# Routing attention chunks in groups of up to four, with row factors made on chip and another order of the last ranks

## The chip, the cores and the metric

One core of a Trainium2 chip. The metric is the device time of one execution in microseconds (us). A core has five engines that each work through their own queue in order: PE (matmuls), DVE (vector operations), ACT (activations and copies), POOL (general vector work and indirect DMA) and SP (which here only issues DMA). An engine that reaches an instruction whose input isn't ready waits, and everything behind it in its queue waits too.

## The reference, cut to what matters

```python
# 1. linear attention with decay: 4 batches, 8 heads, 768 tokens, 64 dims
state = gamma * state + k_t v_t^T;  y_t = scale * q_t state      # per batch and head
x = y.transpose(0, 2, 1, 3).reshape(3072, 512)
# 2. mixture of experts, one expert of 8 for each token
logits = x @ w_gate;  e_idx = argmax(logits)
gate_w = softmax(logits)[e_idx];  eom = sigmoid(x @ w_output_gate)[e_idx]
out[token] = gate_w * eom * (relu(x[token] @ w1[e_idx]) @ w2[e_idx])
# 3. a gated MLP (512 -> 1536 -> 512) on rms-normalised rows
```

## The kernel before, in words

The kernel has three stages: attention with routing (0 to 173 us of the trace), the experts, and the second MLP. The change is in the first stage alone.

**Attention** runs over 24 chunks of 128 tokens, `CPB` = 6 to a batch. The loop over `n` does, in this order: `load(n + 3)` (SP loads 1 MB of q, k and v into one of four `qkv` buffers), `vscale(n + 1)` (POOL makes `vt`, L451), `qk(n + 1)` (PE L467, then two masked copies `am` on DVE, L474), `rows(n - 1)`, `qs_pv(n)` (PE L490, which reads the state `st`, and L495; DVE multiplies by the row factors `rs` into `xt`, L500), `st_up(n)` (PE L513; half of the state is copied out by ACT, L517, and after it the other half by DVE, L518), and `place(n - 1)`. The first chunk of a batch has no L490, the last no L513.

**Rows and routing.** `rows(n)` multiplies `xt` by weights and gate columns (PE L524); DVE adds up the 16 logits `lg` (L529) and ACT copies the 512-wide `row` out of PSUM (L532). Then the chunk is routed, one chunk at a time: a maximum, a comparison, a second maximum, a one-hot `ohb` and the running counts (DVE, L539 to L544), the exponentials (ACT L545, L549), and in `place` the rank in the expert (PE L555 to L557, three small matmuls), the gate and the slot number (DVE L558 to L565). `place` ends with a multiply of the row by its gate (ACT L588), its store to DRAM (DMA issued by ACT, L589) and a scatter of token numbers into the list `lst` (POOL L579).

**Weights beside it.** After every second chunk an expert's weight tile is split in two parts: ACT copies the high part (L179) and POOL subtracts it (L180, 128x1024).

**The last chunks.** Tokens of the first expert tile are gathered from DRAM by four indirect DMAs (L255). Those of the last three chunks are not stored and gathered but multiplied in by a one-hot matrix (`direct_in`, PE L595, which needs `pt`, `rh` and `rl` of `place`); the gathered ones are transposed (`settle_in`, PE L604). Then come the splits (ACT L263, DVE L264) and the first expert matmul, L285.

The order within each engine is the order of the code; there is no scheduler. Tiles are guarded by semaphores.

Of the kernel before, what the change touches and what calls it, by code (L numbers as in the profile page):

```python
# [9 lines left out]
F32 = mybir.dt.float32  # L10
# [34 lines left out]
EARLY = 4  # L45
SETTLED = 4
# [12 lines left out]
A_END = A_IDS + NCH  # L59
# [12 lines left out]
def shape_constants():  # L72
    g = 1.0 - 2.0 ** (-5.0 - np.arange(H, dtype=np.float64))
    p = np.arange(128)
    c = np.zeros((128, C_END))
    c[:, C_ID:C_ID + 128] = np.eye(128)
    c[:, C_EPS] = 1e-6
    c[:, C_MID] = -1024.0
    a = np.zeros((128, A_END))
    a[:, A_MASK:A_MASK + 128] = p[:, None] <= p[None, :]  # L80
    a[:, A_U:A_U + 128] = p[:, None] < p[None, :]
    t = np.arange(CPB)[None, :, None] * CH + p[:, None, None] + 1.0
    a[:, A_VS:A_VS + CPB * H] = (g[None, None, :] ** (-t)).reshape(128, -1)
# [5 lines left out]
    rs = g[hd] ** ti / np.sqrt(D)  # L89
# [14 lines left out]
def fused_kernel(  # L104
# [311 lines left out]
    with ExitStack() as es:  # L416
# [3 lines left out]
        rp = pool(es, "rowp", 4)  # L420
# [7 lines left out]
        e3 = ap.tile([128, 8], BF16, name="e3")  # L428
# [5 lines left out]
        junk = ap.tile([128, 4, NE], F32, name="junk")  # L434
        prio = ca[:, A_PRIO:A_PRIO + 8]

        a_t, vt_t, am_t, xt_t, row_t, rt, direct = {}, {}, {}, {}, {}, {}, {}
# [82 lines left out]
        def rows(n):  # L520
            xt = xt_t.pop(n)
            for k in range(KB):
# [3 lines left out]
            t = rp.tile([128, DM], F32, name="row", tag="row")  # L526
            row_t[n] = t
            lg = tp.tile([128, 16], F32, name="lg", tag="lg")
            DVE.tensor_reduce(  # L529
                out=lg, in_=v[:, :, :, 128:144].rearrange("p a b j -> p j a b"), axis=AX.XY, op=ALU.add  # L530
# [4 lines left out]
            sc = tp.tile([128, 12], F32, name="sc", tag="sc")  # L535
            col = [sc[:, i:i + 1] for i in range(12)]
            mx, pm, nmx, sm, nz, ez, s1, t1, gw, pos = col[:10]
            ohb = tp.tile([128, NE], BF16, name="ohb", tag="ohb")
            DVE.tensor_reduce(out=mx, in_=lg[:, 0:8], axis=AX.X, op=ALU.max)  # L539
            DVE.scalar_tensor_tensor(out=junk[:, 0], in0=lg[:, 0:8], scalar=mx, in1=prio, op0=ALU.is_ge, op1=ALU.mult)  # L540
            DVE.tensor_scalar(out=nmx, in0=mx, scalar1=-1.0, scalar2=None, op0=ALU.mult)
            DVE.tensor_reduce(out=pm, in_=junk[:, 0], axis=AX.X, op=ALU.max)
            DVE.tensor_scalar(out=ohb, in0=prio, scalar1=pm, scalar2=None, op0=ALU.is_equal)
            DVE.tensor_tensor(out=run_cnt[:, n + 1], in0=run_cnt[:, n], in1=ohb, op=ALU.add)  # L544
            ACT.activation(out=junk[:, 1], in_=lg[:, 0:8], func=AF.Exp, bias=nmx, accum_out=sm)  # L545
            DVE.scalar_tensor_tensor(
                out=junk[:, 2], in0=lg[:, 8:16], scalar=-1.0, in1=ohb, op0=ALU.mult, op1=ALU.mult, accum_out=nz
            )
            ACT.activation(out=ez, in_=nz, func=AF.Exp)  # L549
            rt[n] = (ohb, ez, sm, s1, t1, gw, pos)  # L550

        def place(n):
            ohb, ez, sm, s1, t1, gw, pos = rt.pop(n)
            rk = ps[:, 7, (n % 2) * 8:(n % 2) * 8 + 8]
            PE.matmul(rk, lhsT=oh[0:1], rhs=e3[0:1], start=True, stop=False)  # L555
            PE.matmul(rk, lhsT=oh, rhs=run_cnt[:, n], start=False, stop=False)
            PE.matmul(rk, lhsT=uh, rhs=ohb, start=False, stop=True)  # L557
            DVE.tensor_scalar(out=s1, in0=sm, scalar1=1e-9, scalar2=None, op0=ALU.add)  # L558
            DVE.tensor_scalar(out=t1, in0=ez, scalar1=1.0, scalar2=s1, op0=ALU.add, op1=ALU.mult)
            DVE.scalar_tensor_tensor(  # L560
                out=junk[:, 3], in0=rk, scalar=1.0, in1=ohb, op0=ALU.mult, op1=ALU.mult, accum_out=pos
            )
            DVE.reciprocal(out=gw, in_=t1)
            ii = tp.tile([128, 1], I32, name="ii", tag="ii", bufs=3)
            DVE.tensor_copy(out=ii, in_=pos)  # L565
            t = row_t.pop(n)
            if n >= NCH - NDIRECT:
                pt = dp.tile([128, CAPS[0]], F32R, name="pt", tag="pt")
                DVE.tensor_scalar(out=pt, in0=slots, scalar1=pos, scalar2=None, op0=ALU.is_equal)
                rh = dp.tile([128, DM], F32R, name="rh", tag="rh")  # L570
                rl = dp.tile([128, DM], F32R, name="rl", tag="rl")
                ACT.activation(out=rh, in_=t, func=AF.Copy, scale=gw)
                DVE.scalar_tensor_tensor(out=rl, in0=t, scalar=gw, in1=f32(rh), op0=ALU.mult, op1=ALU.subtract)
                direct[n] = (pt, rh, rl)
            if n < NCH - 1:
                store_row(n, t, gw)
            else:
                row_t[n] = (t, gw)
            ins = POOL.indirect_dma_start(  # L579
                out=lst[:, :], out_offset=bass.IndirectOffsetOnAxis(ap=ii, axis=0), in_=ids[:, n:n + 1], in_offset=None  # L580
# [19 lines left out]
        def settle_in(ks):  # L600
            for k in ks:
                for t0 in range(0, CAPS[0], 128):
                    r = min(128, CAPS[0] - t0)
                    PE.matmul(  # L604
                        ps[:, k, t0:t0 + r], lhsT=xw[0:r, t0 // 128, k * 128:(k + 1) * 128], rhs=ident[0:r, 0:r],
                        start=False, stop=True, skip_group_check=True,
                    )
# [44 lines left out]
        SP.dma_start(out=rs[:, 0], in_=rsc[:, 0])  # L652
# [5 lines left out]
        SP.dma_start(out=rs[:, 1], in_=rsc[:, 1])  # L658
# [3 lines left out]
        DVE.tensor_copy(out=e3, in_=ca[:, A_E3:A_E3 + 8])  # L662
# [8 lines left out]
        ex = Experts(None, None, None, None, None)  # L671
        for n in range(NCH):
# [394 lines left out]
```

## Time and profile before

| what | value |
|---|---|
| median of 3 runs | 1124.92 us (1124.22 to 1126.25) |
| the profiled execution | 1119.29 us, of which its span is 1117.2 us |
| mean granted TensorE clock | 0.986 of full speed |
| busy, share of the span | PE 94%, DVE 49%, ACT 34%, POOL 30% |
| first expert matmul (L285) | at 173.34 us of the span |

Times in the trace are counted from the span's start. The profiled execution is 5.63 us faster than the median of the runs; 2.1 us of its time lie outside the span. A row of a timeline gives start, duration, engine, line and operation, and in brackets how long its engine had been idle and what ended that. The view by windows gives the busy time of each engine in a stretch, then the granted clock, the DMA share and GB/s.

### The profile page before, as it was taken

Reading aid. Unit: us, or ns where it says so; the run is one execution under the profiler, and the core shown is the slowest. Engines: PE = TensorE matmul, PEld = TensorE weight load, DVE = VectorE, ACT = ScalarE, POOL = GpSimd, SP = SyncE. Lnnn points to the kernel's source line nnn. Section 1 sums busy time; section 2 is a strip of 40 time slices with the busy share of each in tenths; the row PEclk is TensorE's granted clock in tenths of the full one; section 3 lists DMA queues with packets and bytes.
Section 4 is the critical chain, followed back from the end, with each engine's and each line's share of the span. In section 5 each row is a group of like instructions: output and inputs, shape, how many; then the busy total and the mean of one; then the engine's idle time right before and its main releaser. Section 6 shows DMA issues by size and latency. Waiting matters only on the chain.

```text
span 1117.2 us, 16379 instructions
## 1 busy us (share of the span) xinstructions
PE 1055.5 (94%) x6393; PEld 982.8 (88%) x6394; DVE 550.9 (49%) x1045; ACT 381.4 (34%) x721; POOL 337.2 (30%) x271
## 2 busy tenths in 40 slices
PE   7788889999999999989899899999999999999995
PEld 6687779989999999978788799999999999999995
DVE  4699963256666676888888831111311112211111
ACT  1344333444444544555555531111311112211111
POOL 3355544556466656332433310000110000200002
PEclk9899989999999999999999999999999999999998
DMA  8999724445446555543343220000210000100001
GB/s 301 229 307 284 204 63 135 123 135 197 155 142 205 182 156 155 171 104 94 114 141 114 85 85 29 1 1 1 64 50 1 1 1 30 57 1 1 1 1 60
DMA packets 47864, 116.74 MB, mean 104 GB/s; under 512 B 12966, under 2 KB 24486, under 8 KB 44962
## 3 DMA queue, kind: packets, MB, share of 16 engines
q1 hardware_dynamic: 39602, 97.05, 28.8%
q0 software_dynamic: 4864, 12.53, 3.2%
q10 hardware_dynamic: 3312, 6.03, 1.6%
q8 instruction: 52, 0.85, 0.3%
q14 instruction: 34, 0.28, 0.1%
HBM read 93.06 MB, written 23.11 MB: 104 GB/s over the span
## 4 chain that ended last, share of the span: by engine, by line
issue 43%; PE 25%; DVE 11%; POOL 3%; DMA 2%; ACT 2%; POOLq 0%; DVEq 0%; SPq 0%; ACTq 0%
PE ps L285 12%; PE ps L298 11%; DVE fb L226 2%; DVE fb L229 2%; POOL out_dram L780 2%; DVE fu L232 1%; DVE fb L223 1%; PE ps L271 1%; DMA out_dram<-ob,perm 1%; DVE a L755 1%; DVE al L757 1%; ACT ah L756 1%; DVE ys L347 1%; PE ps L604 1%; DMA raw<-wm 1%
## 5 line engine op out<-in xcount | busy, mean ns | idle before, releaser
L747 PE MATMUL ps<-zh,w 128*128 128x384 f32 x960 | 255.2, 336 | 2.6 <-DVE hl L292 1.3
L755 DVE TENSOR_TENSOR a<-a,ps 128x384 f32<-128x384 f32 x96 | 52.8, 550 | 320.2 <-PE ps L747 317.7
L180 POOL TENSOR_TENSOR w<-raw,w 128x1024 fp32r<-128x1024 f32 x64 | 154.7, 2426 | 103.0 <-ACT w L179 102.2
L747 PEld LDWEIGHTS ps<-zh,w 128*128 128x128 f32 x960 | 174.6, 188 | 5.7 <-ACT a L754 1.7
L747 PE MATMUL ps<-xh,w 128*128 128x384 f32 x576 | 156.5, 341 | 9.8 <-ACT a L754 7.2
L747 PE MATMUL ps<-zl,w 128*128 128x384 f32 x480 | 161.2, 336 | 0.0
L285 PE MATMUL ps<-xh,w 128*128 128x448 f32 (+7 forms) x512 | 149.6, 353 | 0.1
L765 PE MATMUL ps<-w,ah 128*128 128x512 f32 x564 | 145.5, 393 | 0.2 <-ACT ys L320 0.2
L780 POOL DMA_INDIRECT out_dram<-xw,perm x10 | 9.9, 992 | 423.3 <-ACT xw L778 420.1
L756 ACT ACTIVATE ah<-a 128x384 fp32r<-128x384 f32 x94 | 49.3, 525 | 209.6 <-DVE a L755 209.6
L747 PEld LDWEIGHTS ps<-xh,w 128*128 128x128 f32 x576 | 104.9, 188 | 17.3 <-ACT a L754 11.3
L765 PEld LDWEIGHTS ps<-w,ah 128*128 128x128 f32 x564 | 104.7, 188 | 16.6 <-ACT ys L320 0.6
L754 ACT ACTIVATE a<-ps 128x384 f32<-128x384 f32 x96 | 46.7, 487 | 202.6 <-PE ps L747 202.5
L298 PE MATMUL ps<-hh,w 128*128 128x448 f32 (+7 forms) x512 | 106.6, 350 | 0.0
L285 PEld LDWEIGHTS ps<-xh,w 128*128 128x128 f32 x512 | 95.2, 188 | 3.4
L747 PE MATMUL ps<-xl,w 128*128 128x384 f32 x288 | 96.9, 336 | 0.0
L298 PEld LDWEIGHTS ps<-hh,w 128*128 128x128 f32 x512 | 93.8, 188 | 2.9
L747 PEld LDWEIGHTS ps<-zl,w 128*128 128x128 f32 x480 | 90.1, 188 | 2.3
L285 PE MATMUL ps<-xl,w 128*128 128x448 f32 (+7 forms) x256 | 89.8, 351 | 0.0
L180 POOL TENSOR_TENSOR w<-fu,w 128x512 fp32r<-128x512 f32 x36 | 55.7, 1546 | 111.7 <-ACT w L179 108.2
L765 PE MATMUL ps<-w,al 128*128 128x512 f32 x282 | 80.1, 392 | 0.0
L757 DVE TENSOR_TENSOR al<-a,ah 128x384 fp32r<-128x384 f32 x94 | 52.5, 558 | 55.5 <-ACT ah L756 55.5
(154 smaller groups left out, 1497.9 us busy)
## 6 DMA issues: line engine op xcount, KB each, us to landing
raw<-wmoe SPq DMA_DIRECT2D x64, 512.0 KB, 3.9
qkv<-att SPq DMA_DIRECT2D x22, 1024.0 KB, 8.0
raw<-wm SPq DMA_DIRECT2D x36, 512.0 KB, 3.7
xw<-z SPq DMA_DIRECT2D x8, 768.0 KB, 6.4
xr<-row ACTq DMA_DIRECT2D x23, 256.0 KB, 7.8
z<-ys SPq DMA_DIRECT2D x2, 912.0 KB, 7.6
z<-ys SPq DMA_DIRECT2D x2, 896.0 KB, 4.3
z<-ys SPq DMA_DIRECT2D x2, 864.0 KB
```

Source lines behind the costliest of these rows:

```text
L180: POOL.tensor_tensor(out=dst[:, 1, c], in0=src, in1=f32(dst[:, 0, c]), op=ALU.subtract)
L226: DVE.scalar_tensor_tensor(out=b, in0=lo, scalar=29, in1=b, op0=ALU.logical_shift_right, op1=ALU.bitwise_or)
L229: DVE.scalar_tensor_tensor(out=b, in0=hi, scalar=-(1 << 30), in1=b, op0=ALU.bitwise_and, op1=ALU.bitwise_or)
L285: PE.matmul(p, lhsT=wtile[:, s, k * 128:(k + 1) * 128], rhs=x[w % len(xh)][:, k, 0:n], start=(i == 0), stop=(i == 3 * KB - 1),)
L298: PE.matmul(ps[:, 4 + k, 0:n], lhsT=wtile[:, s, 512 + k * 128:512 + (k + 1) * 128], rhs=h, start=(f == 0 and j == 0), stop=(f == NF - 1 an ...
L747: PE.matmul(ps[:, part, 0:BT], lhsT=w2(f, part, s, k * 128, (k + 1) * 128), rhs=zz[:, k], start=(i == 0), stop=(i == 3 * KB - 1),)
L754: ACT.activation(out=a, in_=ps[:, 0, 0:BT], func=AF.Silu)
L755: DVE.tensor_tensor(out=a, in0=a, in1=ps[:, 1, 0:BT], op=ALU.mult)
L756: ACT.activation(out=ah, in_=a, func=AF.Copy)
L757: DVE.tensor_tensor(out=al, in0=a, in1=f32(ah), op=ALU.subtract)
L765: PE.matmul(ps[:, o_bank[b % 2][t]], lhsT=x[:, t * 128:(t + 1) * 128], rhs=w2(f, 2, s, 0, 512), start=(f == 0 and j == 0), stop=(f == NF2 ...
L780: ins = POOL.indirect_dma_start(out=out[:, :], out_offset=bass.IndirectOffsetOnAxis(ap=pm[:, t0 + t], axis=0), in_=o, in_offset=None, boun ...
```

## The change

1. **Groups.** `rows` no longer routes. When the last chunk of a group has its logits, `route` makes a list of steps for the whole group, each step one instruction over up to four chunks (128x32 in place of 128x8), only the running counts one by one. Groups are 4, 4, 4, 4, 3, 2, 2 and 1 chunks. A group of four has 14 steps in a first part and eight in a second, then one `place` per chunk.
2. **Pumps.** The steps wait in a list `todo`. Each iteration takes five of them after `qk(n + 1)` and six after `qs_pv(n)`, 40 from iteration 20 on. For a group of four that ends at chunk e, iteration e+1 has the first six steps, e+2 eleven, e+3 the last of the steps and then all four `place`, ahead of `st_up(e + 3)`.
3. **Formulas.** The accumulated sums of two instructions become reductions of their own, and the exponentials get their maximum subtracted by DVE. A group of four has 19 DVE instructions of routing, a chunk before had 14.
4. **Buffers.** Seven row buffers in place of four; three are tiles that the later stages use.
5. **Row factors.** Five of the six 256 KB loads of `rs` fall away; `rs` of chunk c is the first one times a factor per partition and head pair, four ACT instructions of 128x128 for each c, in iterations 0 to 4.
6. **The last ranks.** `rows` and the first part of the route of chunk 23 stand ahead of all `direct_in`; `settle_in` goes by gathered tiles of 128 tokens (before by blocks of 128 columns); `direct_in` of chunk 22 stands ahead of it.

ACT from the row copy of one iteration (`L532` before, `L542` after) over the stores to the next row copies. Before, over one iteration:

```order
L532 ACTIVATE row<-ps 128x512
L545 ACTIVATE junk,sc<-lg,sc 128x8
L549 ACTIVATE sc<-sc 128x1
L517 ACTIVATE st_134<-ps 64x4x64
L588 ACTIVATE row<-row,sc 128x512
L589 DMA xr<-row 128x512
L532 ACTIVATE row<-ps 128x512
```

After, iteration 6, in which the group of chunks 0 to 3 is placed:

```order
L542 ACTIVATE fu_72<-ps 128x512
L618 ACTIVATE row_136<-row_136,gw_all 128x512
L619 DMA xr<-row_136 128x512
L618 ACTIVATE row_137<-row_137,gw_all 128x512
L619 DMA xr<-row_137 128x512
L618 ACTIVATE row_138<-row_138,gw_all 128x512
L619 DMA xr<-row_138 128x512
L618 ACTIVATE row_139<-row_139,gw_all 128x512
L619 DMA xr<-row_139 128x512
L528 ACTIVATE st_134<-ps 64x4x64
```

Before, the copy of the state stands ahead of one store in each iteration; now it stands behind four in every fourth.

DVE over one iteration. Before, every iteration reads like this (`sc` holds the small values of one chunk):

```order
L474 TENSOR_TENSOR am_661<-ps,ca 128x512
L529 TENSOR_REDUCE lg<-ps 128x16
L539 TENSOR_REDUCE sc<-lg 128x1
L540 SCALAR_TENSOR_TENSOR junk<-lg,sc,ca 128x8
L541 TENSOR_SCALAR sc<-sc 128x1
L542 TENSOR_REDUCE sc<-junk 128x1
L543 TENSOR_SCALAR ohb<-ca,sc 128x8
L544 TENSOR_TENSOR run_cnt<-run_cnt,ohb 128x8
L546 SCALAR_TENSOR_TENSOR junk,sc<-lg,ohb 128x8
L500 TENSOR_TENSOR xt<-ps,rs 128x512
L518 COPY st_133<-ps 64x4x64
L558 TENSOR_SCALAR sc<-sc 128x1
```

After, iteration 6 from its masked copies on (`s_all` is the product under the gate, `gw_all` the gate, `ii_all` the slot number):

```order
L485 TENSOR_TENSOR am_516<-ps,ca 128x512
L583 SCALAR_TENSOR_TENSOR s_all<-sm_all,t_all 128x4
L586 RECIPROCAL gw_all<-s_all 128x4
L556 TENSOR_TENSOR junk_143<-ps,ohb 128x32
L559 TENSOR_REDUCE pos_all<-junk_143 128x4
L589 CAST ii_all<-pos_all 128x4
L539 TENSOR_REDUCE lg<-ps 128x16
L511 TENSOR_TENSOR xt<-ps,rs 128x512
L529 COPY st_134<-ps 64x4x64
```

The gates of four rows are now made ahead of the logits `lg` and of `xt` of that iteration; the iteration behind it has no routing steps.

PE at the end of the attention. Before, between the first `settle_in` and the first expert matmul:

```order
L604 MATMUL ps<-cs,xw 128x128 x3
L604 MATMUL ps<-cs,xw 128x64
L555 LDWEIGHTS oh
L555 MATMUL ps<-e_129,oh 128x8
L556 LDWEIGHTS oh
L556 MATMUL ps<-run_cnt,oh 128x8
L557 LDWEIGHTS uh
L557 MATMUL ps<-ohb,uh 128x8
L604 MATMUL ps<-cs,xw 128x128 x3
L604 MATMUL ps<-cs,xw 128x64
```

After, from the last matmul of chunk 22's `direct_in` on:

```order
L625 MATMUL ps<-pt,rl 128x448
L635 MATMUL ps<-cs,xw 128x128 x8
L562 LDWEIGHTS oh
L562 MATMUL ps<-e_129,oh 128x8
L563 LDWEIGHTS oh
L563 MATMUL ps<-run_cnt,oh 128x8
L564 LDWEIGHTS uh
L564 MATMUL ps<-ohb,uh 128x8
L635 MATMUL ps<-cs,xw 128x128 x4
L635 MATMUL ps<-cs,xw 128x64 x4
L625 MATMUL ps<-pt,rh 128x448
```

The eight matmuls of `direct_in(22)` moved from behind the gathered transposes to ahead of them; the last rank stays between the halves, which are now halves of the tokens.

The core of the diff:

```diff
+GMAX = 4
+GROUPS = [4, 4, 4, 4, 3, 2, 2, 1]
...
+        row_bufs = [rp.tile([128, DM], F32, name=f"row{i}") for i in range(4)] + fl_u + [f32(fl_b[0])]
...
+            first = [
+                red(mx[:, r], lg[:, r, 0:8], ALU.max),
+                tt(j0, lg[:, r, 0:8], mx[:, r].to_broadcast(shape), ALU.is_ge),
+                tt(j0, j0, pr, ALU.mult),
+                red(pm[:, r], j0, ALU.max),
+                tt(ohb[:, r], pr, pm[:, r].to_broadcast(shape), ALU.is_equal),
+                *[tt(run_cnt[:, n + 1], run_cnt[:, n], ohb[:, n], ALU.add) for n in range(n0, n0 + g)],
+                tt(j1, lg[:, r, 0:8], mx[:, r].to_broadcast(shape), ALU.subtract),
+                lambda: ACT.activation(out=j1, in_=j1, func=AF.Exp),
+                tt(j2, lg[:, r, 8:16], ohb[:, r], ALU.mult),
+                red(nz[:, r], j2, ALU.add),
+                lambda: ACT.activation(out=ez[:, r], in_=nz[:, r], func=AF.Exp, scale=-1.0),
+            ]
+            second = [
+                rank,
+                red(sm[:, r], j1, ALU.add),
+                lambda: DVE.tensor_scalar(out=t1[:, r], in0=ez[:, r], scalar1=1.0, scalar2=None, op0=ALU.add),
+                lambda: DVE.scalar_tensor_tensor(
+                    out=s1[:, r], in0=sm[:, r], scalar=1e-9, in1=t1[:, r], op0=ALU.add, op1=ALU.mult
+                ),
+                lambda: DVE.reciprocal(out=gw[:, r], in_=s1[:, r]),
+                tt(j3, rk.rearrange("p (g e) -> p g e", g=g), ohb[:, r], ALU.mult),
+                red(pos[:, r], j3, ALU.add),
+                lambda: DVE.tensor_copy(out=ii[:, r], in_=pos[:, r]),
+                *[lambda n=n: place(n) for n in range(n0, n0 + g)],
+            ]
+            return first, second
...
+                ACT.activation(out=rs[:, c, a], in_=rs[:, 0, a], func=AF.Copy, scale=ca[:, k:k + 1])
...
         for n in range(NCH):
             load(n + 3)
-            if 2 <= n + 2 < CPB:
-                SP.dma_start(out=rs[:, n + 2], in_=rsc[:, n + 2])
...
             qk(n + 1)
+            if n + 1 < CPB:
+                row_scales(n + 1)
+            pump(5)
             if n >= 1:
-                rows(n - 1)
+                routed_rows(n - 1)
             qs_pv(n)
+            pump(6 if n < NCH - 4 else 40)
             st_up(n)
-            if 1 <= n < NCH - 1:
-                place(n - 1)
...
+        routed_rows(NCH - 1)
+        pump(11)
         direct_in(NCH - 3, True)
-        place(NCH - 2)
-        rows(NCH - 1)
+        direct_in(NCH - 2, False)
         settle_in((0, 1))
-        place(NCH - 1)
+        pump(40)
         settle_in((2, 3))
-        direct_in(NCH - 2, False)
         direct_in(NCH - 1, False)
```

`place` loses its rank and gate steps and keeps the scaled row, the store and the scatter.

## Rows read from the trace of the kernel before

**Rows 1.** Windows: busy us of each engine (instructions), granted clock, DMA share, GB/s.

```profile
56.00:84.00 28.00, 24.71 (x327) 22.35 (x322) 26.16 (x90) 12.38 (x30) 15.21 (x17) 1.00 0.98 309
...
196.00:224.00 28.00, 28.00 (x146) 25.69 (x146) 8.13 (x12) 13.24 (x21) 15.08 (x8) 1.00 0.42 127
```

**Rows 2.** Timeline of PE: one iteration without a wait, chunk 21 to 22.

```profile
131.51 1.16 PE L467 MATMUL ps<-qkv 64*128 64x128 f32 x16
...
133.68 1.05 PE L490 MATMUL ps<-qkv,st 128*128 128x128 f32 x8
134.67 1.09 PE L495 MATMUL ps<-am,vt 128*64 128x128 f32 x16
135.59 0.63 PE L513 MATMUL ps<-vt,qkv 128*64 128x64 f32 x16
136.16 0.17 PE L555 MATMUL ps<-e,oh 1*128 1x8 bf16 x1
...
136.40 1.16 PE L467 MATMUL ps<-qkv 64*128 64x128 f32 x16
```

**Rows 3.** DVE in the stretch 0 to 175 us, by line and shape: busy us, mean ns.

```profile
L474 DVE TENSOR_TENSOR am<-ps,ca 128x512 f32<-128x512 f32 x48 | 30.7, 682 | 17.9 <-PE ps L467 17.8
...
L518 DVE COPY st<-ps 64x256 f32<-64x256 f32 x20 | 8.6, 428 | 2.8 <-ACT st L517 2.3
...
L539 DVE TENSOR_REDUCE sc<-lg 128x1 f32<-128x8 f32 x24 | 3.9, 161 | 0.8
```

**Rows 4.** Timelines of POOL and DVE: a split, and two routing steps.

```profile
135.78 2.34 POOL L180 TENSOR_TENSOR w<-raw,w 128x1024 fp32r<-128x1024 f32 x1 [0.87 <-ACT w L179]
138.08 1.04 POOL L451 TENSOR_TENSOR vt<-qkv,ca 128x512 f32<-128x512 f32 x1
...
135.81 2.32 DVE L544 TENSOR_TENSOR run_cnt<-run_cnt,ohb 128x8 bf16<-128x8 bf16 x1
...
156.55 0.23 DVE L540 SCALAR_TENSOR_TENSOR junk<-lg,sc,ca 128x8 f32<-128x8 f32 x1
```

**Rows 5.** Timeline of PE: three starts of L467 (chunks 5, 7, 9).

```profile
32.29 1.16 PE L467 MATMUL ps<-qkv 64*128 64x128 f32 x16
...
50.20 2.08 PE L467 MATMUL ps<-qkv 64*128 64x128 f32 x16 [6.88 <-DMA qkv<-att]
...
61.78 1.16 PE L467 MATMUL ps<-qkv 64*128 64x128 f32 x16
```

**Rows 6.** Waits of SP's queue, 0 to 180 us: us in total, times, longest.

```profile
SPq L445 <- DMA xr<-row: 11.0, 2, 6.5
```

**Rows 7.** DMA issues of the page: times issued, KB, median us to landing.

```profile
qkv<-att SPq DMA_DIRECT2D x22, 1024.0 KB, 8.0
```

**Rows 8.** Timeline of ACT: one row's multiply, and what follows its store's issue.

```profile
86.01 0.72 ACT L588 ACTIVATE row<-row,sc 128x512 f32<-128x512 f32 x1 [1.04 <-DVE ii L565]
...
87.13 1.06 ACT L179 ACTIVATE w<-raw 128x1024 fp32r<-128x1024 f32 x1 [0.40 <-ACT row L588]
```

**Rows 9.** ACT in the stretch 0 to 175 us, by line and shape.

```profile
L532 ACT ACTIVATE row<-ps 128x512 f32<-128x512 f32 x24 | 14.2, 591 | 23.5 <-DVE lg L529 22.6 <-DVE ohb L543 0.5 <-DVE sc L542 0.5
...
L517 ACT ACTIVATE st<-ps 64x256 f32<-64x256 f32 x20 | 7.3, 364 | 1.9 <-PE ps L513 1.9
```

**Rows 10.** A wait of PE in its timeline, and the window of 4 us behind it.

```profile
113.94 0.17 PE L557 MATMUL ps<-ohb,uh 128*128 128x8 bf16 x1 [1.75 <-DVE ohb L543]
...
117.28 1.92 PE L490 MATMUL ps<-qkv,st 128*128 128x128 f32 x8
...
116.00:120.00 4.00, 4.00 (x28) 3.78 (x28) 3.76 (x18) 1.71 (x4) 2.11 (x3) 0.57 0.81 234
```

**Rows 11.** The end of the attention: timelines of DVE and PE.

```profile
152.97 0.69 DVE L500 TENSOR_TENSOR xt<-ps,rs 128x512 f32<-128x512 f32 x1
...
160.77 3.60 PE L604 MATMUL ps<-cs,xw 128*128 128x128 f32 x12 [1.17 <-DMA xw<-xr,ix]
...
173.34 0.47 PE L285 MATMUL ps<-xh,w 128*128 128x448 f32 x1
```

More of the change, by code (lines that the diff above doesn't have):

```diff
@@ L58 @@
 A_IDS = A_E3 + 8
-A_END = A_IDS + NCH
+A_STEP = A_IDS + NCH
+A_END = A_STEP + (CPB - 1) * NP
 T_KEY = 0
@@ L534, in rows @@
             )
[L535 to L548, printed above, removed]
@@ L549, in rows, with route, tt, red @@
-            ACT.activation(out=ez, in_=nz, func=AF.Exp)
-            rt[n] = (ohb, ez, sm, s1, t1, gw, pos)
-        def place(n):
[L553 to L566, printed above, removed]
+        def route(n0, g):
+            r = slice(n0, n0 + g)
+            shape = [128, g, NE]
+            j0, j1, j2, j3 = [j[:, 0:g] for j in junk]
+            c0 = GMAX * NE * (n0 % 2)
+            rk = ps[:, 7, c0:c0 + NE * g]
+            pr = prio.to_broadcast(shape)
+            def tt(out, in0, in1, op):
+                return lambda: DVE.tensor_tensor(out=out, in0=in0, in1=in1, op=op)
+            def red(out, in_, op):
+                return lambda: DVE.tensor_reduce(out=out.rearrange("p g o -> p (g o)"), in_=in_, axis=AX.X, op=op)
+            def rank():
+                PE.matmul(rk, lhsT=oh[0:1], rhs=e3[0:1, 0:g].rearrange("p g e -> p (g e)"), start=True, stop=False)
+                PE.matmul(rk, lhsT=oh, rhs=run_cnt[:, r].rearrange("p g e -> p (g e)"), start=False, stop=False)
+                PE.matmul(rk, lhsT=uh, rhs=ohb[:, r].rearrange("p g e -> p (g e)"), start=False, stop=True)
+            first = [
[23 more added lines that the diff above has]
+                *[lambda n=n: place(n) for n in range(n0, n0 + g)],
+            ]
+            return first, second
@@ L567, in place @@
+        def place(n):
+            t, w = row_t.pop(n), gw[:, n]
             if n >= NCH - NDIRECT:
                 pt = dp.tile([128, CAPS[0]], F32R, name="pt", tag="pt")
-                DVE.tensor_scalar(out=pt, in0=slots, scalar1=pos, scalar2=None, op0=ALU.is_equal)
+                DVE.tensor_scalar(out=pt, in0=slots, scalar1=pos[:, n], scalar2=None, op0=ALU.is_equal)
                 rh = dp.tile([128, DM], F32R, name="rh", tag="rh")
                 rl = dp.tile([128, DM], F32R, name="rl", tag="rl")
-                ACT.activation(out=rh, in_=t, func=AF.Copy, scale=gw)
@@ L573, in place @@
-                DVE.scalar_tensor_tensor(out=rl, in0=t, scalar=gw, in1=f32(rh), op0=ALU.mult, op1=ALU.subtract)
+                ACT.activation(out=rh, in_=t, func=AF.Copy, scale=w)
+                DVE.scalar_tensor_tensor(out=rl, in0=t, scalar=w, in1=f32(rh), op0=ALU.mult, op1=ALU.subtract)
                 direct[n] = (pt, rh, rl)
             if n < NCH - 1:
-                store_row(n, t, gw)
+                store_row(n, t, w)
             else:
-                row_t[n] = (t, gw)
+                row_t[n] = (t, w)
@@ L598, in direct_in, with settle_in @@
                     )
[L600 to L603, printed above, removed]
+        def settle_in(ts):
+            for t in ts:
+                t0 = t * 128
+                r = min(128, CAPS[0] - t0)
+                for k in range(KB):
                     PE.matmul(
-                        ps[:, k, t0:t0 + r], lhsT=xw[0:r, t0 // 128, k * 128:(k + 1) * 128], rhs=ident[0:r, 0:r],
+                        ps[:, k, t0:t0 + r], lhsT=xw[0:r, t, k * 128:(k + 1) * 128], rhs=ident[0:r, 0:r],
                         start=False, stop=True, skip_group_check=True,
@@ L651, in fused_kernel @@
         POOL.memset(nowhere, NT)
-        SP.dma_start(out=rs[:, 0], in_=rsc[:, 0])
+        SP.dma_start(out=rs[:, 0], in_=rsc)
         SP.dma_start(out=iwt, in_=iw)
@@ L661, in fused_kernel @@
         DVE.tensor_copy(out=ones, in_=oh)
-        DVE.tensor_copy(out=e3, in_=ca[:, A_E3:A_E3 + 8])
+        DVE.tensor_copy(
+            out=e3, in_=ca[:, A_E3:A_E3 + 8].rearrange("p (o e) -> p o e", o=1).to_broadcast([128, GMAX, 8])
+        )
         DVE.tensor_copy(out=ids, in_=ca[:, A_IDS:A_IDS + NCH])
@@ L671, in fused_kernel, with row_scales, routed_rows, pump @@
         ex = Experts(None, None, None, None, None)
+        def row_scales(c):
+            for a in range(NP):
+                k = A_STEP + (c - 1) * NP + a
+                ACT.activation(out=rs[:, c, a], in_=rs[:, 0, a], func=AF.Copy, scale=ca[:, k:k + 1])
+        ends, todo = {}, []
+        for i, g in enumerate(GROUPS):
+            ends[sum(GROUPS[:i + 1]) - 1] = g
+        def routed_rows(n):
+            rows(n)
+            if n in ends:
+                g = ends[n]
+                for part in route(n - g + 1, g):
+                    todo.extend(part)
+        def pump(n):
+            for step in todo[:n]:
+                step()
+            del todo[:n]
         for n in range(NCH):
             load(n + 3)
-            if 2 <= n + 2 < CPB:
-                SP.dma_start(out=rs[:, n + 2], in_=rsc[:, n + 2])
             for o, i in fill.get(n, ()):
```

27 lines of the change are left out of this document (16 added, 11 removed).

## The prediction

> **What bounds the kernel now.** I read four views in this order. The windows first: from 196 us on PE is busy in every microsecond (28.00 of 28), and the order of the engines from the first expert matmul on is the same before and after, so whatever the change gives or costs is decided by when that matmul starts, 173.34 us [rows 1, 11]. In 56 to 84 us nothing is full but DVE (26.16 of 28) and the DMA share (0.98); PE has 24.71, ACT 12.38. Second, the timeline of PE where nothing holds it: one iteration from L467 to L467 takes 4.89 us, 0.24 of it the rank, so 4.65 without; the read of the state (L490) starts 2.17 us into it [rows 2]. Third, the starts of L467: from chunk 5 to 9 they are 29.49 us apart, 6.88 of it one wait for a load, and from chunk 9 to 21 it is 69.73 us, 5.81 each [rows 2, 5]. The load came late because SP waited for row stores, 11.0 us in two waits [rows 6]. Fourth, what makes 5.81 out of 4.89: DVE. Its two masked copies take 1.36 us, and a step with two inputs in SBUF stretches from 0.23 to 2.32 us when POOL's weight split of 2.34 us runs beside it [rows 3, 4]. So DVE sets the pace of the attention, PE is 0.9 us behind it, and one load stall stands on top.
>
> **The steps, part by part.** All sums are made on the profiled execution (1119.29 us) and then set on the median of the runs, 1124.92, since only differences are summed.
>
> *Groups: the relief.* Per chunk DVE had 14 routing instructions; now 19 serve four. At 0.16 to 0.25 us a step [rows 3, 4] a group needs some 4 us of DVE instead of 13, and DVE no longer fills the iteration. PE's 4.65 us becomes the pace wherever nothing else stalls.
>
> *Groups: the first six steps.* They stand between `xt` and DVE's half of the state copy. POOL's `vt` (1.04 us [rows 4]) starts when the matmuls before it free its buffer, just as the comparison begins, so I count its whole length: 1.3 + 0.9 us of steps, of which PE's distance to L490 hides all but 0.4. The eleven steps of the next iteration are hidden but for the rank on PE, 0.24 [rows 2].
>
> *Groups: the placing.* Here lies the cost. Let U be the start of L467 in iteration e+3. ACT's state half ends late (U+1.4) because the row copy and an exponential precede it; DVE's half is done at U+1.8 (0.43 [rows 3]), the two masked copies at U+3.1. Now the product under the gate, two inputs in SBUF, is next; the split, after its ACT part of 1.06 us [rows 8], runs from U+2.5 to U+4.85 and holds it as the split of rows 4 held L544. Five steps of 0.15 to 0.25 end at U+5.75, the logits at U+5.95. ACT's row copy waits for the logits (22.6 of its 23.5 us idle were that [rows 9]) and takes 0.59, to U+6.55. Then come four rows at 1.12 us each (from one multiply to the instruction behind the issue, 86.01 to 87.13 [rows 8]): U+11.05. Only then ACT's state half, 0.36 [rows 9], and DVE's, 0.43: U+11.85. PE wants it at U+4.65+2.17 = U+6.8. **PE loses 5.0 us in each group**; one store an iteration never cost this, since each lay behind the state's copy.
>
> *The four groups, chunk 5 to 21.* 4 x 4.65 + 0.4 + 0.24 + 5.0 = 24.25 for a group. Chunks that end or begin a batch take off 0.6 in three groups and 1.0 in one (where the placing follows at once, the shorter step only lengthens the stall): 23.65 three times and 23.25, in all 94.2. Before it was 131.51 - 32.29 = 99.22 [rows 2, 5]. Gain 5.0, which is the load stall of 6.88 less a loss of 1.9: with the first stores in iteration 6 and no `rs` loads, the load of chunk 7 has nothing to wait for.
>
> *Chunk 21 to 23.* Before 152.97 - 131.51 = 21.46 [rows 2, 11]. From iteration 20 on a whole rest of a group is pumped at once: iteration 20 three stores behind two exponentials, a stall of 4.1; iteration 21 the full chain of a group of two, whose rank stands on PE ahead of L513 and waits some 2.1 for seven DVE steps, then a stall of 2.5 behind two stores. 3 x 4.65 + 8.7 + 3.1 to the last L495, with one rank more, 0.9 in all for the ranks and slips, is 26.75. Loss 5.3.
>
> *The tail.* Before, from the last `xt` to the first expert matmul 20.37 us; the gathered rows had come only at 160.77, and the last rank, its direct rows and two `direct_in` all followed [rows 11]. Now the chain of chunk 23 sets it: `xt` 0.7, the chain of chunks 21 and 22 4.2, their direct rows 2.6, the first part for chunk 23 2.4, the second 1.7, its direct rows 1.9, eight matmuls 1.65, the split 1.25: 16.4. Gain 4.0; 2 if the gathers come as late against `xt` as their scatters now do, 6 if the chains overlap.
>
> *Row factors.* Five loads less help the start little, since PE there runs on the chunk loads issued ahead of them: 0 to 0.8, I take 0.4. The 20 ACT instructions of 128 columns cost at most 0.36 each, the price of 256 columns [rows 9], 1.4 us in an iteration in which ACT has more than half its time free [rows 1]; without that cover it would be 7.
>
> *The clock.* A PE wait of 1.75 us was followed by a window of 4 us at a granted clock of 0.57: L490 took 1.92 us in place of 1.05, so 4 x 0.43 = 1.7 us were lost [rows 2, 10]. Stalls of 4 to 5 us come in four groups and twice at the end, close together: I count five, 8.5 us.
>
> Sum: +5.0 - 5.3 + 4.0 + 0.4 - 8.5 = -4.4, slower by 4.4: 1123.7 against the profiled 1119.29, and 1129 against the median.
>
> **A rule of the skill beside it.** The trace shows a two-input DVE step held for the whole of the split (L544, 2.32 beside 2.34) [rows 4]. The Trainium skill, "SBUF — State Buffer", section "Who interferes with whom", tells this as an exclusive lock of a port pair that DVE and GpSimd share: the instruction that issues first holds it to its end, "Issue order, not op shape, decides who blocks". By it the change would be worse off in kind, since ten of a group's 19 steps have two SBUF inputs (three of 14 before), and better off wherever a step gets in before the split; that second result is weighed as rival 2.
>
> **Rivals.**
> 1. *The clock holds.* From 56 to 84 us PE idled 3.3 us in all at a granted clock of 1.00 [rows 1], so not every wait costs clock; if these don't, the 8.5 falls away: 1120.8. Against it: 1.75 us were enough once [rows 10].
> 2. *The gate is ready in time.* If the masked copies are done before U+2.5, the product precedes the split, which then waits 0.25 us. That takes 1.75 off a group, and ACT's state half of e+2, not late by an exponential, takes off another 0.65 or so: a stall of 2.6, 4 x 2.4 = 9.6 less. 1119.7, faster than before. It decides by 0.6 us in my schedule, so it is near. By the skill's rule on the issue order alone, 4 x 1.75 = 7.0 would come off, 1122.3; no row shows the split itself held.
> 3. *Half of that*: the product waits, but the state is copied early, or the reverse. 1124.5, no change.
> 4. *Loads come late.* At 4.65 us an iteration a load issued two iterations ahead has 9.3 us to land, and its median is 8.0 with DMA at 0.98 already [rows 1, 7]; four stores at once stand in the same queues. Two waits of 1 us in each group would be 8 us more: 1137.
> That the relief isn't there at all is no rival of weight: DVE's row of 26.16 of 28 can't be read otherwise. That every stall is hidden would give some 1109; I see no row for it.
>
> **How the numbers follow.** My sum as it stands (1127.2 to 1134) 0.37; rival 1 0.13; rival 2 0.19; rival 3 0.17; rival 4 0.14. Faster by over 0.2% (2.25 us, about what a measurement of this kernel can tell from no change: below 1122.7) is rivals 1 and 2: 0.32; within 0.2% rival 3 and the edge of the first: 0.19; slower 0.49. The likeliest is 1129. Around it the sum's own ends are 1127 and 1134; the range reaches to rival 2 with a tail at 6 us, and to rival 4: 1115 to 1138.
>
> **What the profile after will show.** Right: in iterations 6, 10, 14 and 18 four pairs of multiply and issue ahead of ACT's state copy, L490 (now L501) waiting for that copy some 5 us, the granted clock at half behind it; no 6.9 us wait for a load near 43 us; iterations without a stall at 4.65. The product under the gate at 1.5 us or more would show the split's hold, at 0.2 rival 2. The first expert matmul then starts at 177 to 178 us. Wrong: L501 waiting under 3 us, PE at full clock through the attention, or PE waiting for `qkv` in most iterations.

## The result and the profile after

| | before | after |
|---|---|---|
| median | 1124.91 us (1124.22 to 1126.25) | 1138.97 us (1136.64 to 1140.86) |
| ratio | | 1.0126, 95% interval 1.0106 to 1.0146 |
| profiled execution | 1119.29 us | 1140.86 us |
| granted clock | 0.986 | 0.968 |
| first expert matmul | 173.34 us | 195.25 us |

The change costs 14.1 us by the medians. The two profiled executions lie 21.6 us apart, because that of before is faster than any other run of its kernel and that of after is the slowest of its four. All of the difference between the traces stands ahead of the first expert matmul, 195.25 - 173.34 = 21.9. By stretches in us, from starts of the first matmul of a chunk (L467 before, L478 after); `xt` is the tile that DVE makes for the rows:

| stretch | before | forecast | after |
|---|---|---|---|
| start to chunk 5 | 32.29 | 31.9 | 32.09 |
| chunk 5 to 21 | 99.22 | 94.2 and 6.8 of clock | 117.53 |
| chunk 21 to the last `xt` | 21.46 | 26.75 and 1.7 of clock | 27.94 |
| last `xt` to the first expert matmul | 20.37 | 16.4 | 17.69 |

Only the second row is far off, by 16.5 us. The windows of after that answer to [rows 1] (busy us of PE, PEld, DVE, ACT and POOL with their instructions, granted clock, DMA share, GB/s):

```profile
56.00:84.00 28.00, 23.20 (x273) 20.97 (x269) 14.28 (x39) 9.74 (x17) 13.65 (x15) 0.87 0.95 195
84.00:112.00 28.00, 19.68 (x215) 17.55 (x211) 12.71 (x35) 6.76 (x13) 12.03 (x14) 0.80 0.94 232
112.00:140.00 28.00, 20.81 (x221) 18.54 (x223) 12.70 (x38) 5.99 (x11) 9.18 (x8) 0.85 0.95 153
```

DVE did fall, from 26 to 13 or 14 us of 28, and PE didn't gain: it has less than before, at a lower clock. The DMA share is as high as before while the bytes moved fell from 309 to 195 GB/s. Those two columns and the granted clock are where the answer lies.

The first placing, in iteration 6, in the timelines of after (start, duration, engine, line, idle before and its end). PE, which feels it at the start of iteration 7:

```profile
45.56 1.16 PE L478 MATMUL ps<-qkv 64*128 64x128 f32 x16
48.18 1.22 PE L535 MATMUL ps<-iwt,xt 128*128 128x144 f32 x8 [1.46 <-ACT fu L542]
53.37 2.08 PE L501 MATMUL ps<-qkv,st 128*128 128x128 f32 x8 [3.96 <-DVE st L529]
```

DVE and POOL, then ACT:

```profile
44.21 2.10 DVE L583 SCALAR_TENSOR_TENSOR s_all<-sm_all,t_all 128x4 f32<-128x4 f32 x1
...
52.88 0.43 DVE L529 COPY st<-ps 64x256 f32<-64x256 f32 x1 [4.85 <-ACT st L528]
...
43.93 2.35 POOL L184 TENSOR_TENSOR w<-raw,w 128x1024 fp32r<-128x1024 f32 x1 [5.94 <-ACT w L183]
...
47.97 0.71 ACT L618 ACTIVATE row<-row,gw_all 128x512 f32<-128x512 f32 x1
...
52.48 0.38 ACT L528 ACTIVATE st<-ps 64x256 f32<-64x256 f32 x1 [0.40 <-ACT row L618]
```

This is the forecast chain: the product under the gate held by the split (2.10 beside 2.35), four rows of 1.13 us each on ACT (start to start), then the state. PE lost 1.46 + 3.96 = 5.4, and ran L501 at half speed behind it (2.08 in place of 1.05). What the forecast sum didn't have are these, waits of PE for chunk loads:

```profile
70.38 1.16 PE L478 MATMUL ps<-qkv 64*128 64x128 f32 x16 [1.29 <-DMA qkv<-att]
...
91.89 1.16 PE L478 MATMUL ps<-qkv 64*128 64x128 f32 x16 [2.92 <-DMA qkv<-att]
...
134.09 2.08 PE L478 MATMUL ps<-qkv 64*128 64x128 f32 x16 [4.05 <-DMA qkv<-att]
```

### The profile page after: what moved, and what is told of

The parts are those of the page before. It is cut to its first block, busy times and chain, and to the rows that moved or that the text cites. A ratio compares the mean times of both kernels' runs of the same rounds, so it can differ in the third digit from the quotient of the medians.

```text
span 1139.0 us, 15993 instructions
## 1 busy us (share of the span) xinstructions
PE 1065.7 (94%) x6345; PEld 992.2 (87%) x6346; DVE 515.9 (45%) x853; ACT 378.6 (33%) x685; POOL 336.7 (30%) x271
## 4 chain that ended last, share of the span: by engine, by line
issue 43%; PE 29%; DVE 13%; DMA 7%; ACT 4%; POOL 3%; ACTq 1%; SPq 0%; POOLq 0%; DVEq 0%
PE ps L289 11%; PE ps L302 11%; DMA qkv<-att 3%; DVE fb L230 2%; DVE fb L233 2%; POOL out_dram L834 2%; DVE fu L236 1%; PE ps L501 1%; DVE fb L227 1%; PE ps L506 1%; PE ps L275 1%; DMA out_dram<-ob,perm 1%; DVE a L809 1%; PE ps L478 1%; DVE al L811 1%
## 5 line engine op out<-in xcount | busy, mean ns | idle before, releaser
L819 PEld LDWEIGHTS ps<-w,ah 128*128 128x128 f32 x564 | 104.7, 188 | 16.5 <-ACT ys L324 0.5
```

What stands on the lines that cost most here:

```text
L819: PE.matmul(ps[:, o_bank[b % 2][t]], lhsT=x[:, t * 128:(t + 1) * 128], rhs=w2(f, 2, s, 0, 512), start=(f == 0 and j == 0), stop=(f == NF2 ...
```

## The experiments

Each kernel below is the changed one or the one before with the edit shown. Times are medians in us, with the ratio to the kernel before on the same chip and its 95% interval. "5 to 21" is the stretch from chunk 5 to chunk 21 in the profiled execution.

| run | median | ratio, interval | 5 to 21 |
|---|---|---|---|
| before | 1124.9 | | 99.2 |
| after | 1139.0 | 1.0126 (1.0106 to 1.0146) | 117.5 |
| four places behind the state | 1147.2 | 1.0181 (1.0120 to 1.0243) | 118.4 |
| splits in even iterations | 1136.3 | 1.0091 (1.0062 to 1.0119) | 117.9 |
| row factors alone, on before | 1123.5 | 0.9984 (0.9958 to 1.0009) | 101.8 |
| places spread | 1125.6 | 1.0023 (1.0001 to 1.0044) | 100.2 |
| scatters together, rows spread | 1131.2 | 1.0067 (1.0038 to 1.0096) | 102.5 |
| groups of two | 1129.0 | 1.0037 (1.0013 to 1.0062) | 111.4 |
| after, scatters spread | 1126.8 | 1.0025 (1.0007 to 1.0043) | 107.2 |
| groups of two, spread | 1123.9 | 1.0001 (0.9983 to 1.0019) | 102.9 |
| after without scatters | 1124.0 | 0.9995 (0.9982 to 1.0008) | 103.9 |
| the same, places behind the state | 1095.7 | 0.9762 (0.9741 to 0.9783) | 81.7 |
| before without scatters | 1092.7 | 0.9728 (0.9708 to 0.9748) | 86.6 |
| before with each scatter twice | 1185.0 | 1.0542 (1.0509 to 1.0576) | 151.8 |
| before, scatters late | 1127.6 | 1.0023 (0.9995 to 1.0051) | 100.2 |
| places spread, scatters late | 1131.1 | 1.0037 (1.0008 to 1.0066) | 99.2 |
| before, scatters graded | 1126.4 | 1.0010 (0.9989 to 1.0032) | 95.9 |

### Is it the order on ACT?

Theory Q: the state's copy behind four stores. Theory D: stores and scatters at once make the chunk loads late. In the first run the four places move behind `st_up`:

```diff
             st_up(n)
+            places(40)
```

> The changed kernel with one edit: the four places of a group (row multiply, store, scatter) stand behind st_up of the same iteration, so that ACT copies the state out ahead of the four stores. Theory Q (ACT's queue): the waits of PE for the state (18.5 us in 8 times) and most of the half clock behind them go, while the stores stay together; about 1115 to 1121. Theory D (DMA): four stores and scatters at once make the chunk loads late, and PE waits for them all the same: the load waits stay at 8 us or grow, the clock falls behind them, 1126 to 1133.

It came out at 1147.2, above both ranges and certainly no faster (its interval and that of the changed kernel overlap). The waits of PE and then of ACT in 20 to 200 and 20 to 180 us (us, times, longest):

```profile
PE ps L478 <- DMA qkv<-att: 12.8, 4, 5.7
PE ps L535 <- issue: 8.1, 6, 2.7
PE ps L535 <- ACT fu L542: 7.7, 3, 3.8
PE ps L535 <- ACT row L542: 3.5, 1, 3.5
PE ps L501 <- DVE st L529: 3.4, 4, 1.5
...
ACT fu L542 <- DMA xr<-fu: 15.1, 2, 10.5
...
ACT row L542 <- DMA xr<-row: 10.9, 2, 6.9
```

The wait for the state is gone (18.5 to 3.4), and its place is taken by loads and by row copies whose buffer still waits for a store to land. So theory Q alone falls: what PE gained at the state went into waits for DMA. What the 8.1 us are that the profile puts down to "issue", in the middle of groups of matmuls, stays open.

The rival on the split, tested by moving the splits to the other iterations:

```diff
-            if n >= 3 and n % 2 == 1:
-                convs_to((n - 3) // 2)
-                loads_to((n - 3) // 2 + 2)
+            if n >= 4 and n % 2 == 0:
+                convs_to((n - 4) // 2)
+                loads_to((n - 4) // 2 + 2)
```

> The changed kernel with one edit: the weight splits (ACT and POOL) follow the even iterations instead of the odd ones, so that no split runs beside the product under the gate in the iterations in which a group is placed. Everything else is left. If the split's hold sets the gate's time, the product takes 0.2 us in place of 2.1, the wait for the state shrinks by 1.8 in each of four groups, and the time falls by 7 to 9 us against the changed kernel, to 1130 to 1132. If the stores alone set it, there is no difference: 1137 to 1140.

The product under the gate took 152 ns each time, and in the changed kernel 1131 ns in the mean of four (two held, two not). The median is 2.7 lower, between the two expectations; the two intervals overlap, so that a gain isn't shown. PE's load waits from 32 to 150 us rose from 8.3 to 13.4 us.

Of the small parts, the row factors alone, put into the kernel before:

```diff
-            if 2 <= n + 2 < CPB:
-                SP.dma_start(out=rs[:, n + 2], in_=rsc[:, n + 2])
...
+            if n + 1 < CPB:
+                row_scales(n + 1)
```

> The kernel before with one part of the change: five loads of row factors left out, the factors made by 20 ACT instructions in iterations 0 to 4. If the early load stall (6.9 us) came from those loads, it goes: 1118 to 1120. If it came from the row stores that share the queues' semaphores, it stays and the time is that of before within 1.5 us; if ACT's 20 instructions are not hidden, up to 6 us more.

No measurable difference. SP no longer waited for row stores, yet PE still waited 4.05 us for the load of chunk 7 (6.88 in [rows 5]), and all its load waits from 20 to 200 us were 13.2 us, against 9.6 before. SP's wait for row stores, to which I had put the stall down, was a part of it at most.

### Stores or scatters?

One place in each iteration:

```diff
             st_up(n)
+            places(1 if n < 18 else 2 if n < 20 else 40)
```

> The changed kernel with one place in each iteration behind st_up (two from iteration 18, the rest from 20 on), seven row buffers as in the change. The run with all four places behind st_up stood at 1147 with 20.6 us of load waits, 11 of PE waits for row copies and 26 us of ACT waits for stores to land, so theory Q (ACT's queue) alone has fallen. Theory D (stores and scatters together choke the DMA): the load waits behind the start (some 12 us) fall under 4, no row copy waits for a store, 1110 to 1120. If the loads are late because PE's faster pace alone asks for too much: load waits stay at 8 us or more, 1125 to 1140.

1125.6: nearly all of the loss is gone, but nothing is gained. PE's waits for loads stay at 7.8, just under the bound of the second case, and 16.4 us go to row copies, where the first case had none. (An eighth row buffer finds no room: the kernel's next pool needs 17.25 KB of each partition, and 16.16 are left.) ACT, 20 to 180 us:

```profile
ACT row L542 <- DMA xr<-row: 30.7, 7, 6.8
...
ACT fu L542 <- DMA xr<-fu: 12.5, 2, 9.3
```

The same, with the rows spread but the scatters of a group together:

```diff
             places(1 if n < 18 else 2 if n < 20 else 40)
+            scatters()
```

> As the spread run, but the four scatters of a group are issued together on POOL as in the change, only the row multiplies and stores are one for each iteration. If the stores side by side choke the DMA: as fast as the spread run, within 2 us. If the scatters do: the load waits of the changed kernel come back, 8 us or more, and the time is 1128 to 1142.

1131.2, 5.6 more than with all spread, but the runs vary widely (1125.6 to 1141.1), and in the profiled execution, one of the fastest, the chunk loads cost PE only 1.8 us, not the expected 8, and row copies 19.6. That leans to the scatters, without settling it. Then the changed kernel without its scatters; the list then holds only its fill, which lies out of range, so that the gathers fetch nothing either (the expectation has this wrong), and the stretch from chunk 5 to 21, ahead of the gathers, is the better comparison:

```diff
-            ins = POOL.indirect_dma_start(
-                out=lst[:, :], out_offset=bass.IndirectOffsetOnAxis(ap=ii[:, n], axis=0), in_=ids[:, n:n + 1],
...
```

> The changed kernel without any scatter of token numbers (the list keeps its fill, so the gathers fetch one row over and over); stores stay four together ahead of the state's copy. If the scatters choke the DMA: GB/s behind the stores stay over 250, load waits behind the start go (8 us and their clock), 1120 to 1127, only the waits for the state stay. If the stores do: no difference in the attention, 1135 to 1141, the first expert matmul at 193 to 196 us.

The waits for the state are still all there, and no wait for a load is left. PE from 32 to 150 us:

```profile
PE ps L501 <- DVE st L529: 20.9, 9, 4.0
PE ps L535 <- ACT row L542: 1.7, 2, 1.5
```

How the four stores of the first group leave is seen in the DMA view of 12 us (40 equal slices of it, busy tenths and GB/s), first the changed kernel, 52 to 64 us:

```profile
DMA  9997699699899455989999999007972579962909
GB/s 356 342 158 34 48 55 82 55 82 103 61 96 68 27 27 41 89 75 75 96 157 82 69 61 89 7 7 82 191 62 14 55 41 61 137 48 27 69 0 144
DMA packets 556, 1.01 MB, mean 84 GB/s; under 512 B 133, under 2 KB 133, under 8 KB 534
...
q10 hardware_dynamic: 455, 0.82, 88.0%
...
q0 software_dynamic: 79, 0.00, 1.1%
```

and without scatters, 50 to 62 us:

```profile
DMA  9999999723000000000000000904579999983000
GB/s 382 403 417 403 389 362 396 273 89 68 0 0 0 0 0 0 0 0 0 0 0 0 0 0 0 300 0 109 191 273 410 437 437 437 410 355 137 0 0 0
DMA packets 670, 2.00 MB, mean 167 GB/s; under 512 B 84, under 2 KB 84, under 8 KB 541
...
q10 hardware_dynamic: 520, 0.93, 20.2%
```

Without scatters the same stores move at 360 to 420 GB/s and are done in some 3 us. Behind four scatters all traffic together moves at 84 GB/s in the mean of these 12 us, at a share of 1.12 (0.47 without): the engines are occupied, and move little. Queue q10 carries the row stores (packets, MB, share): theirs are the packets that take the time, 88.0% for 0.82 MB against 20.2% for 0.93 MB. The scatters' own, in q0, take 1.1%, so that the price stands in another queue's row. Each scatter writes 128 numbers of 4 bytes. The Trainium skill, "DMA: Bandwidth & Descriptors", section "Specifications", says of transfers below 512 B that they are done as a read-modify-write; the size of these writes agrees, but no run here shows that this is the cause.

The cross-check keeps the four stores ahead of the state and spreads only the scatters:

```diff
             st_up(n)
+            scatters(1 if n < 18 else 2 if n < 20 else 40)
```

> The changed kernel with the same scatters, but one in each iteration (two from iteration 18); the four stores stay together ahead of the state's copy. If the clustering of the scatters makes the loads late: load waits behind the start under 3 us (8.3 in the changed kernel), stores land in under 10 us, 1126 to 1131. If the number of scatters matters and not their clustering: 1135 to 1141.

1126.8, the load waits from 8.3 to 2.9 us, as expected. So of the 14 us of the change 11 to 12 (by the ratios and by the medians) go when the four scatters no longer stand side by side. PE's waits for the state are all still there, 17.7 us from chunk 5 to 21 where the changed kernel has 15.6. The spread run above has 1.7 of them and the same time within 1.2 us: with the scatters in it, the kernel gains nothing measurable from an earlier copy of the state.

Half-sized groups lie between, 1129.0:

```diff
-GROUPS = [4, 4, 4, 4, 3, 2, 2, 1]
+GROUPS = [2, 2, 2, 2, 2, 2, 2, 2, 2, 1, 2, 2, 1]
```

> The changed kernel with groups of two instead of four (the last ones as before: 1, 2, 2, 1); with two chunks the places fall into the pump ahead of the rows, two stores at a time ahead of the state's copy. Theory D: the load waits and the waits for the state shrink by more than half, 1122 to 1130. If clustering is not the cause but the lag of the stores or the number of buffers: 1135 or more.

Its time fell by 10 us, and the waits for the state to 4.2 us, but PE's load waits, 26.4 us from 20 to 200 us in its profiled execution, did not: on them the expectation failed. Why two scatters at a time leave more of them than four is open, and speaks against reading the load waits as the price of clustering alone.

### What do the scatters cost the kernel before?

The same lines are left out of the kernel before, and in another run doubled:

```diff
+            ins2 = POOL.indirect_dma_start(
+                out=lst2[:, :], out_offset=bass.IndirectOffsetOnAxis(ap=ii, axis=0), in_=ids[:, n:n + 1], in_offset=None
+            )
```

> The kernel before without any scatter of token numbers, as the changed kernel without them, which fell by 15 us to 1124. If the scatters cost the kernel before just as much, it falls by 10 to 15 us to 1110 to 1115, and they explain nothing of the difference of the two. If they hurt only when four come together, it falls by less than 6 us: its pace is set by DVE, and one scatter an iteration is hidden.

> The kernel before with each scatter done twice, the second time into a list of its own that nobody reads. Taking the scatters away gave 31.6 us, so if the DMA behind them paces the attention of the kernel before, as much or more is lost again: 1150 to 1180, with loads and stores that land later than 7.7 us and waits of PE for loads. If what was gained came from POOL's time or from the gathers of one row, little changes: 1124 to 1132.

Without them the kernel before falls by 31.6 us, more than either expectation, of which the gathers that fetch nothing have a part; from chunk 5 to 21, ahead of the gathers, it is 99.2 - 86.6 = 12.6 us. With each scatter twice it rises by 60.7 us, 2.5 us for each of the 24, and PE waits for loads (0 to 240 us; 53.0 of it from chunk 5 to 21):

```profile
PE ps L468 <- DMA qkv<-att: 59.9, 15, 14.1
```

The price of a scatter is more than POOL's 1.0 us, and it isn't one number: 12.6 us for the 16 chunks of the stretch when the only one is left out, 52.6 when a second is added. Where the 12.6 lie is seen in PE's waits from chunk 5 to 21, first the kernel before, then without scatters:

```profile
PE ps L467 <- DMA qkv<-att: 9.6, 4, 6.9
PE ps L524 <- DVE xt L500: 6.5, 5, 1.7
PE ps L557 <- DVE ohb L543: 3.6, 6, 1.8
...
PE ps L524 <- DVE xt L500: 8.6, 7, 1.7
PE ps L557 <- DVE ohb L543: 1.5, 1, 1.5
PE ps L467 <- DMA qkv<-att: 1.3, 1, 1.3
```

Waits for loads fall by 8.3; waits for DVE are 10.1 in both; the rest is PE's busy time, 79.5 and 75.0 us, at a granted clock of 0.95 and 1.00. So up to chunk 10, where those load waits stand, the kernel before is held by DMA, and behind it by DVE. That POOL is freed too shows in none of these waits.

Without scatters and with the places behind `st_up`, the two edits together, the changed kernel shows what its grouping is worth:

> The changed kernel without scatters and with the four places behind st_up: both suspected causes gone. The waits for the state were 21.6 us in the run without scatters; if they cost what they show, with the clock behind them, this falls by 20 to 26 us against that run's 1124, to 1098 to 1104. If less than 10 us are gained, something else paces PE.

```profile
30.23 1.16 PE L478 MATMUL ps<-qkv 64*128 64x128 f32 x16
...
111.94 1.16 PE L478 MATMUL ps<-qkv 64*128 64x128 f32 x16
```

81.7 us, against 103.9 with the state's wait: four placings cost 22.2, 5.6 each with the clock behind them. By the medians the order on ACT is now worth 28.3 us (1124.0 to 1095.7), where with the scatters it was worth nothing. Against the 86.6 of the kernel before without scatters it is 4.9 us better. That is all that the change's relief of DVE gives here, and the end of the attention takes it back: from chunk 21 to the first expert matmul 39.0 us (150.94 - 111.94), in the kernel before without scatters 31.5 (148.93 - 117.39).

### Can the price be avoided?

Groups of two with one place in each iteration, both edits as shown above:

> Groups of two, one place in each iteration behind st_up. A row then lives four iterations to its store in place of six, so the seven buffers cover a store's landing. The spread run lost 16.4 us of PE time to row copies that waited for landings; with these gone 1110 to 1118, faster than both kernels. If DMA is simply full with a scatter in each iteration, the load waits take their place and it stays at 1121 to 1126.

As fast as before, 1123.9: the row copies no longer wait, loads do (11.6 us). Last, the scatters held back until most loads are done, fully and by degrees, and in the changed kernel with spread rows:

```diff
+            scatters({15: 2, 16: 2, 17: 3, 18: 3, 19: 3, 20: 4, 21: 40, 22: 40}.get(n, 0))
```

> The kernel before with its scatters held back: none until iteration 15, then 2, 2, 3, 3, 3, 4 and the rest of the first 21 in iteration 21. If a scatter's price is paid by the loads and stores beside it: chunk 5 to chunk 15 at the pace of the run without scatters (54.2 us, 63.3 before), the list ready a little late, 1108 to 1118. If the price is intrinsic: what is gained until chunk 15 is lost again in chunks 16 to 23 and in the wait for the gathered rows, 1122 to 1132.

> The changed kernel with one row multiply and store in each iteration behind st_up, and the scatters held back as in the run of the kernel before with late scatters. If the price is paid by the transfers beside them: no row copy waits for a landing until iteration 15, 1108 to 1118. If intrinsic: 1122 to 1135.

> The kernel before with one scatter in every second iteration until 13, then 1, 2, 2, 2, 2, 3 and the rest of the first 21 by iteration 21. If the price is paid by the transfers beside them: half of what full holding back gains before chunk 15 and less lost behind it, 1112 to 1120. If intrinsic: 1121 to 1128.

None is faster. In the first (its profiled execution is the slowest of ten), POOL begins to issue late and SP, which reads the list at 149.81 in the kernel before, reads it later:

```profile
95.30 1.15 POOL L585 DMA_INDIRECT lst<-ids,ii  x1 [0.17 <-DVE ii L565]
...
152.48 0.96 POOL L585 DMA_INDIRECT lst<-ids,ii  x1 [2.97 <-DVE ii L565]
...
164.71 0.38 SPq L248 DMA_DIRECT2D ix<-lst  x1
```

Chunk 5 to 15 took 57.1 us in place of 63.3, chunk 15 to 21 took 43.1 in place of 35.9, and the list came 14.9 later: what was gained ahead of chunk 15 was lost behind it. In these schedules the price was moved with the scatters, not hidden. No version with all its scatters was measurably faster than the kernel before.

## Why the prediction was wrong

Slower was right, in part by luck: the stall that I forecast is there with its size, but while the scatters are in the kernel its removal gains nothing, and what made the change slower is mostly something else. 1138.97 lies just above the range.

The step that failed is the sum for chunk 5 to 21, 94.2 us and 6.8 of clock. It holds no wait for loads (I wrote that the load of chunk 7 has nothing to wait for, and left late loads to rival 4) and nothing for four scatters in a row. PE's busy time with its clock and its waits show the terms. The first three rows are the changed kernel, the same without scatters, and that with the places behind `st_up` too; each from chunk 5 to 21, with PE's busy us, granted clock, DMA share and GB/s:

```profile
32.09:149.62 117.53, 88.33 (x969) 0.85 0.95 214
...
30.48:134.42 103.94, 83.36 (x968) 0.87 0.69 245
...
30.23:111.94 81.71, 73.12 (x969) 1.00 0.85 304
```

and waits of PE in the changed kernel, in the same stretch:

```profile
PE ps L501 <- DVE st L529: 15.6, 7, 4.0
PE ps L478 <- DMA qkv<-att: 8.3, 3, 4.1
PE ps L535 <- ACT fu L542: 2.9, 2, 1.5
PE ps L478 <- issue: 2.1, 2, 1.4
```

The third kernel runs the same matmuls at full clock, so that its 73.1 us is PE's work and what the others have above it is the lower clock (the 74.2 is 94.2 less four waits of 5.0):

| chunk 5 to 21 | forecast | after | after without scatters |
|---|---|---|---|
| PE's work at full clock | 74.2 | 73.1 | 73.1 |
| waits for state, row copies, logits | 20.0 | 18.9 | 20.6 |
| waits for loads | 0 | 8.3 | 0 |
| "issue" | 0 | 2.1 | 0 |
| lower clock | 6.8 | 15.2 | 10.2 |
| together | 101.0 | 117.5 | 103.9 |

- **The four groups.** The miss of 16.5 us is half load waits (with "issue", 10.4) and half clock (8.4), less the 2.2 by which work and state waits came out shorter. The same kernel without scatters took 103.9, within 3 us of the 101.0, and spreading the scatters alone took 11 to 12 us off the whole. So 13.6 of the miss hangs on the scatters. Why a scatter slows the other transfers stays open.
- **What bounds the kernel.** I read DVE's 26.16 of 28 us as the pace and the DMA share of 0.98 beside it as a side remark. DVE was read rightly as far as it goes: without scatters it is as full, 26.68 of 28 from 56 to 84 us. But the kernel before also waits 9.6 us for loads that the scatters make late, and doubled scatters cost 60.7. The row to read was the share together with the GB/s: 0.98 at 309 GB/s [rows 1], where without scatters the same engines moved 360 to 420.
- **The placing.** 5.0 us a group forecast, 5.4 in the first group, 20.6 for all four where no scatter disturbs them. Right. The split held the product in two of four placings, so rival 2 (the gate ready in time) was true half of the time, and it paid little or nothing (the run with the splits moved), since loads were late anyway. The rule of the Trainium skill on the shared port ("SBUF — State Buffer", section "Who interferes with whom") agrees: the same step took 2.10 us where the split had begun, 0.15 in the mean where the splits were moved away.
- **The early load stall.** Its end was forecast and came: no wait for chunk 7. The reason given, SP's wait for row stores [rows 6], is at most a part: with the row factors alone these waits of SP are gone and 4.05 us of the stall stay. Without scatters 1.30 of the 6.88 stay in the kernel before; in the changed kernel the first scatter comes only in iteration 6.
- **The clock.** Forecast 1.7 for each of five stalls. Where only the four placings stall, it cost 10.2 us, 2.6 for each. It fell behind load waits too, of 2.92 (with 1.42 for a row copy) and 4.05 us, not behind the one of 1.29; the granted clock from 56 to 140 us was 0.80 to 0.87.
- **Rival 4, loads come late**, had the right sign and 14% of the chance. Its price, 8 us and 1137, is near what was measured, 8.3 us of load waits; but it laid them to PE's pace and to stores, not to the scatters, and had no clock behind them.
- **The end and the tail.** 26.75 and 1.7 of clock forecast (its terms add up to 26.65), 27.94 measured, the two waits of PE for the counts 1.78 each (2.1 forecast); 16.4 forecast, 17.69 measured:

```profile
166.00 0.17 PE L563 MATMUL ps<-run_cnt,oh 128*128 128x16 bf16 x1 [1.78 <-DVE run_cnt L556]
...
195.25 0.54 PE L289 MATMUL ps<-xh,w 128*128 128x448 f32 x1
```

- **Relief.** PE at 4.65 us an iteration wherever nothing stalls was right from chunk 3 to 6, and too good later: 81.7 us from chunk 5 to 21 with both causes away, 5.1 an iteration.

## What to carry to other kernels

When a step is batched, everything that hangs on it is batched too: price the burst on each queue that it uses, DMA among them, not only the instructions that are saved. A DMA share near 1 whose GB/s are below what the same engines moved elsewhere in the trace is a sign of a bound, and leaving out one kind of transfer finds which kind fills it. Removing one of two waits in a row tells little until the other is gone as well: the places behind the state gained nothing with the scatters in, and 28.3 us without them. And waits have a second price in the clock behind them, which PE's busy time for the same matmuls shows.

## What the runs showed of the hardware that I had not expected

A second scatter of 128 numbers of 4 bytes to DRAM in each chunk of the kernel before cost 2.5 us of its time each (60.7 us for 24 more), most of it waits of PE for loads (53.0 us from chunk 5 to 21, 9.6 before), though POOL is busy with one for 1.0 us. Behind four in a row all traffic together moved at 84 GB/s in the mean of 12 us at a share of 1.12, where without them the same stores moved at 360 to 420 GB/s; the time stood in the packets of the row stores, not in those of the scatters.
